# Asking for single packets in the loads of a streaming attention kernel

## The chip, the cores and the metric

The kernel runs on one core of one Trainium2 chip. The metric is device time in microseconds (us) of one execution. Where a run says 363 us, its profile shows a span of 362 us, because the span is taken from the first to the last instruction.

## The reference, cut to what matters

Two independent problems, A and B, are computed and joined. Each is one decode step of attention with a sliding window, two batches, 16 KV heads of width 128, two query heads for each, and the last 4,096 positions of the cache:

```
q = x @ wq                                   # x: [2, 1, 576], wq: [576, 4096]
k, v = the last W = 4096 positions of k_cache, v_cache   # bf16
p = softmax(q k^T * 128**-0.5)
o = p v
out = o @ wo                                 # wo: [4096, 576]
```

There is one query for each sequence, so every byte of K and V is used for very little arithmetic. K and V are 134 MB, wq and wo 19 MB, 153 MB together. The kernel is a stream of loads with computing beside it.

## The kernel before: the parts that matter

All big loads are issued from SyncE ("sp"), on one queue. K and V of four heads of one batch go into one of four ring slots of 4 MB. In SBUF a slot has 128 partitions of 32 KB, and each partition's 32 KB are contiguous in HBM, so a transfer is 128 rows of 32 KB, eight for each of the 16 DMA engines (the trace has 3,968 records of 32,768 B for 31 such transfers; the last V is cut in three). A transfer is issued when its slot is free (`deps`), and its semaphore counts 16.

```
def issue(key):
    ...
    src = src_t[b, 4 * g:4 * g + 4, Sk - W:Sk, :].rearrange("k (r j) d -> r k j d", j=KJ)
    r = slot_of[key]
    prior = uses[r][:uses[r].index(key)]
    deps = [last_reader[prior[-1]]] if prior else first_deps[r]
    cuts = [(0, KJ, ring_sem[r])]                 # one transfer; the last V is cut in three
    ...
    for c0, c1, sm in cuts:
        def f(e, c0=c0, c1=c1, sm=sm):
            return e.dma_start(ring[:, r, c0 * 128:c1 * 128],
                               src[:, :, c0:c1, :].rearrange("r k j d -> r k (j d)")).then_inc(sm, 16)
        stream_dma[key].append((c0, c1, dma_op("sp", sm, 1, f, deps, ...)))
```

wo is loaded in the same way in pieces of up to 18,432 B a row. wq (36,864 B a row) opens the stream. x is tiny and comes on ScalarE's queue ("act"):

```
x:   e.dma_start(x4[2 * h:2 * h + 2, P, :], probs[P][0][:, 0, :]).then_inc(x_sem[P], 16)     # act
wq:  e.dma_start(ringf[:, P * QW:(P + 1) * QW], src).then_inc(wq_sem[P], 16)                 # sp
```

## Time and profile before

| what | before |
|---|---|
| time, median | 363.09 us |
| DMA rate, mean over the span | 424 GB/s |
| share of 16 DMA engines' span taken by the load queue | 98.7% |
| VectorE busy, TensorE busy | 60%, 66% |

First some lines of the page of the kernel before. The line "DMA" is the busy share of the DMA engines in tenths, one digit for each fortieth of the span. Then come the packet count, the load queue and ScalarE's queue (packets, MB, share of 16 engines' span), and the engines' shares of the chain that ended last.

```profile
DMA  8999999999999999999999999999999999999996
DMA packets 6227, 153.26 MB, mean 424 GB/s; under 512 B 700, under 2 KB 840, under 8 KB 1224
q1 hardware_dynamic: 6196, 153.10, 98.7%
q10 hardware_dynamic: 20, 0.01, 0.0%
DMA 48%; DVE 26%; PE 16%; issue 8%; ACT 1%; POOL 0%; SPq 0%
```

In every slice but the two at the ends the DMA engines are at least 90% busy. The trace's packet records say it more sharply: at every moment from 3 to 357 us at least 16 packets are under way, as many as there are engines. Next, the windows view of the kernel before in four stretches of the stream. A line gives the stretch in us and its length, then the busy us (and instructions) of TensorE, its weight loads, VectorE, ScalarE and GpSimd. The last three numbers are the granted TensorE clock (the share of its full clock that TensorE was allowed in that stretch), the DMA engines' busy share and GB/s.

```profile
25.00:100.00 75.00, 52.08 (x229) 10.72 (x129) 50.95 (x20) 8.44 (x18) 4.72 (x18) 0.89 1.01 433
100.00:200.00 100.00, 65.96 (x361) 16.11 (x267) 61.22 (x38) 15.02 (x24) 5.65 (x20) 0.83 1.00 430
200.00:300.00 100.00, 69.25 (x372) 17.02 (x273) 64.52 (x43) 10.42 (x17) 5.08 (x19) 0.83 1.00 431
300.00:343.00 43.00, 29.36 (x180) 8.14 (x144) 27.16 (x24) 10.00 (x16) 2.07 (x8) 0.80 1.00 428
```

A share of 1.00 or 1.01 at 428 to 433 GB/s: there is no hole in the stream to fill. Last, two groups of the DMA issues of the kernel before (transfers, KB each, median us from issue to landing):

```profile
ring<-in_A_k_cache_dram SPq DMA_DIRECT2D x8, 4096.0 KB, 24.3
ring<-in_A_v_cache_dram SPq DMA_DIRECT2D x8, 4096.0 KB, 29.9
```

At 431 GB/s, 4,096 KB take 9.7 us. A transfer that lands 24 to 30 us after its issue therefore had one or two others ahead of it. The computing keeps the queue filled. The chain's 26% for VectorE lies in stretches in which that queue was still full.

The trace also has the records that the page counts as packets. The 6,196 of the load queue are one for each row (5,506; eight for each engine and transfer) and one for each semaphore write (690 of 4 B, a median 9 ns; 16 for each transfer). From their durations (4,096 B in 159 ns, 36,864 B in 1,364 ns, medians) comes the line rate, 1.177 ns for 32 B, and a constant of 8.4 ns a row. By this estimate, that constant is all of a row's time that joining rows could save.

### The profile page before, as it was taken

How to read it: one execution, taken by the hardware profiler on the slowest of the kernel's cores; microseconds unless marked ns; L12 is line 12 of the kernel's file. 1: busy time of each engine (PE TensorE's matmuls, PEld its weight loads, DVE VectorE, ACT ScalarE, POOL GpSimd, SP SyncE). 2: the span in 40 equal slices, each digit the busy share in tenths (PEclk: the TensorE clock that was granted, in tenths of full speed). 3: DMA queues.
4: the chain of work that ended last, by engine and by line, in shares of the span. 5: the costliest groups of instructions: out<-in, count | busy, mean ns of one | idle time of the engine just before them, and what ended most of it. 6: DMA issues, size and time to landing. Idle time of an engine off the chain costs nothing.

```text
span 361.8 us, 2625 instructions
## 1 busy us (share of the span) xinstructions
PE 240.2 (66%) x1292; PEld 57.2 (16%) x927; DVE 218.7 (60%) x150; ACT 46.0 (13%) x78; POOL 24.3 (7%) x84
## 2 busy tenths in 40 slices
PE   0497787666485747662596675567776875668695
PEld 0000111112111201111121121112112121112222
DVE  1901898495929591934909585682927776674622
ACT  1002100040023000500005000500005000500500
POOL 4200101100010001000010000100010001000000
PEclk9999698969988996888788796888688796868969
DMA  8999999999999999999999999999999999999996
GB/s 327 457 435 406 460 408 446 424 431 438 417 453 408 457 404 428 444 431 431 435 420 444 417 449 410 440 431 438 424 442 412 449 417 429 435 435 431 417 412 256
DMA packets 6227, 153.26 MB, mean 424 GB/s; under 512 B 700, under 2 KB 840, under 8 KB 1224
## 3 DMA queue, kind: packets, MB, share of 16 engines
q1 hardware_dynamic: 6196, 153.10, 98.7%
q8 instruction: 8, 0.13, 0.1%
q14 instruction: 3, 0.02, 0.0%
q10 hardware_dynamic: 20, 0.01, 0.0%
HBM read 153.10 MB, written 0.00 MB: 423 GB/s over the span
## 4 chain that ended last, share of the span: by engine, by line
DMA 48%; DVE 26%; PE 16%; issue 8%; ACT 1%; POOL 0%; SPq 0%
DMA ring<-in_B_k_cache_dram 17%; DVE xt L433 16%; DMA ring<-in_A_k_cache_dram 13%; DMA ring<-in_B_v_cache_dram 9%; DMA ring<-in_B_wq_dram 7%; PE st L264 5%; PE st L459 5%; DMA wob<-in_B_wo_dram 3%; PE pj L264 2%; DVE oR L566 2%; DVE mx L467 2%; DVE pT L506 2%; DVE tmp L559 2%; PE ot L536 2%; PE pj L618 1%
## 5 line engine op out<-in xcount | busy, mean ns | idle before, releaser
L459 PE MATMUL st<-xt,zq 128*128 128x512 bf16 x256 | 124.1, 485 | 86.1 <-DVE xt L433 86.1
L433 DVE STREAM_TRANSPOSE xt<-ring 128x4096 f32<-128x4096 f32 x32 | 141.5, 4427 | 28.0 <-DMA ring<-in_A_k_cache_dram 18.8
L264 PE MATMUL st<-xt,zq 128*128 128x512 bf16 x256 | 122.7, 479 | 0.0
L497 ACT ACTIVATE pR<-st,bias 128x512 bf16<-128x512 f32 x32 | 40.0, 1414 | 222.9 <-DVE bias L490 222.9
L459 PEld LDWEIGHTS st<-xt,zq 128*128 128x128 bf16 x256 | 29.4, 115 | 210.1 <-issue 107.7
L536 PE MATMUL ot<-ring,pT 128*32 128x512 bf16 x512 | 32.6, 396 | 3.9 <-DMA ring<-in_B_v_cache_dram 3.9
L490 DVE SCALAR_TENSOR_TENSOR bias<-vmask,tb,offm 128x4 f32<-128x4 f32 x8 | 1.8, 223 | 43.0 <-PE tb L487 43.0
L520 DVE TENSOR_REDUCE ssum<-tb 128x2 f32<-128x8 f32 x8 | 1.3, 162 | 36.0 <-PE tb L517 36.0
L425 POOL TENSOR_TENSOR zq<-qs,bmask 128x64 bf16<-128x64 bf16 x32 | 8.7, 293 | 168.1 <-PE st L264 145.8
L506 DVE STREAM_TRANSPOSE pT<-pR 128x2048 bf16<-128x2048 bf16 x8 | 18.4, 2303 | 0.8 <-ACT pR L497 0.7
L279 PE MATMUL ot<-ring,pT 128*32 128x512 bf16 x18 | 7.6, 421 | 15.0 <-DMA ring<-in_A_wq_dram 14.2
L559 DVE SCALAR_TENSOR_TENSOR tmp<-ot,rsb,dmask 128x512 f32<-128x512 f32 x16 | 11.5, 719 | 7.9 <-PE ot L536 7.9
L566 DVE TENSOR_REDUCE oR<-tmp 128x128 f32<-128x512 f32 x15 | 15.6, 1042 | 0.5
L536 PEld LDWEIGHTS ot<-ring,pT 128*32 128x32 bf16 x512 | 12.4, 99 | 19.6 <-DMA ring<-in_B_v_cache_dram 5.5
L618 PE MATMUL pj<-wob,oM 128*2 128x288 bf16 x48 | 12.7, 299 | 0.0
L264 PE MATMUL pj<-wob,oM 128*2 128x288 bf16 x48 | 12.7, 299 | 0.0
L264 PE MATMUL pj<-ring,pT 128*32 128x512 bf16 x36 | 11.9, 416 | 0.0
L467 DVE TENSOR_REDUCE mx<-st 128x2 f32<-128x1024 f32 x8 | 9.7, 1213 | 0.1
L497 ACT ACTIVATION_READ_ACCUMULATOR pR<-st,bias 128x1 f32 x32 | 8.8, 276 | 0.0
L264 PE MATMUL st<-ring,pT 128*32 128x512 bf16 x18 | 7.3, 407 | 0.0
L222 DVE TENSOR_TENSOR xt<-xt,hmask 4x1152 bf16<-4x1152 bf16 x2 | 2.7, 1349 | 6.7 <-DMA xt<-in_A_x_dram 6.7
L469 POOL TENSOR_TENSOR mv<-mx,v 128x2 f32<-128x2 f32 x8 | 1.6, 195 | 75.8 <-DVE mx L467 75.8
(68 smaller groups left out, 75.6 us busy)
## 6 DMA issues: line engine op xcount, KB each, us to landing
ring<-in_A_k_cache_dram SPq DMA_DIRECT2D x8, 4096.0 KB, 24.3
ring<-in_A_v_cache_dram SPq DMA_DIRECT2D x8, 4096.0 KB, 29.9
ring<-in_B_k_cache_dram SPq DMA_DIRECT2D x8, 4096.0 KB, 27.0
ring<-in_B_v_cache_dram SPq DMA_DIRECT2D x7, 4096.0 KB, 29.8
ring<-in_A_wq_dram SPq DMA_DIRECT2D x1, 4608.0 KB, 13.3
ring<-in_B_wq_dram SPq DMA_DIRECT2D x1, 4608.0 KB, 23.8
wob<-in_A_wo_dram SPq DMA_DIRECT2D x2, 2304.0 KB, 28.3
wob<-in_B_wo_dram SPq DMA_DIRECT2D x1, 2304.0 KB, 27.4
```

Of the source, the lines that this page charges most:

```text
L264: return e.add_instruction(mybir.InstMatmult(name=nc.get_next_instruction_name(), engine=mybir.EngineType.PE, ins=[e.lower_ap(mv_), e.lowe ...
L279: last = e.matmul(QB[c], wt, mv_, start=first, stop=True, skip_group_check=True)
L425: last = e.tensor_tensor(dst, src, msk, ALU.mult)
L433: Xop[(t, jh)] = dve(lambda e: e.transpose(xt[:, jh, :].bitcast(FP32).rearrange("p (kp x kt) -> p x kp kt", kp=2, kt=2), ring[:, r, jh * H ...
L459: last = e.matmul(ob, wt, mv_, start=first, stop=True, skip_group_check=True)
L467: ch[(G, "max")] = dve(lambda e: e.tensor_reduce(mx[:], st[:, :].rearrange("p (x t) -> p t x", t=2), AX.X, ALU.max), [Sop[(2 * G + 1, 1)]] ...
L497: last = e.activation(pR[:].rearrange("p (x k) -> p k x", k=4)[:, kv, :], st[:, :].rearrange("p (x t) -> p t x", t=2)[:, kv % 2, :], ACTF.Exp,
L506: pT_op[G] = dve(lambda e: e.transpose(pT[:, v, :].rearrange("p (w j q) -> p j w q", w=4, q=8), pR[:].rearrange("p (j w q) -> p j w q", w= ...
L536: last = e.matmul(OTB[32 * c:32 * c + 32, :], pT[:, v, base + 32 * c:base + 32 * c + 32], ring[:, r, jj * 128:(jj + 4) * 128], start=rd == ...
L559: evac_op[i] = dve(lambda e: e.scalar_tensor_tensor(tv, o, rsb[:, v, b:b + 1], dm, ALU.mult, ALU.mult), deps, "ev%d" % i)
L566: ch[(G, "red%d" % b)] = dve(lambda e: e.tensor_reduce(oR[:, b, :], tmp[:].rearrange("p (j d) -> p d j", j=4), AX.X, ALU.add), [evac_op[i] ...
L618: last = e.matmul(PJ[h], oM[:, j, :], mv_, start=start and j == 0, stop=True, skip_group_check=True)
```

## The change

The intent is to have the eight rows that one engine moves for a transfer, and its semaphore write, form one packet in place of nine, to save a cost for each packet. Its whole diff is one keyword in two places, for wo and for K and V. wq is left alone.

```
-    rows[:, j0:j1, :].rearrange("p j n -> p (j n)")).then_inc(sm, 16)
+    rows[:, j0:j1, :].rearrange("p j n -> p (j n)"), single_packet=True).then_inc(sm, 16)
...
-    src[:, :, c0:c1, :].rearrange("r k j d -> r k (j d)")).then_inc(sm, 16)
+    src[:, :, c0:c1, :].rearrange("r k j d -> r k (j d)"), single_packet=True).then_inc(sm, 16)
```

## The prediction

> **What bounds the kernel now.** The DMA engines. The page's DMA row is 9 in nearly every slice, and its queue list gives the one load queue 98.7% of 16 engines' span. The windows view gives a DMA share of 0.96 to 1.05 in every 10 us stretch from 10 us to 350 us, at 408 to 455 GB/s. Transfers of 4,096 KB land a median 24 to 30 us after issue (the DMA issues), though one needs only about 9.7 us at 431 GB/s, so two to three are always queued. VectorE is busy 60%, TensorE 66%; the chain of waits gives 26% to VectorE, but in stretches where the queue is still full. The load queue runs without a hole from 1.7 to 359.2 us; about 2.2 us follow (last matmuls, output store).
>
> **What a packet costs.** In the trace's packet records each row is one record, each completion semaphore another (4 B, 9 ns). Median durations: 4,096 B 159 ns, 32,768 B 1,216 ns, 36,864 B 1,364 ns. From the first and last: 1.177 ns per 32 B plus a constant of 8.4 ns. Of a 32 KB row that is 0.7%; the rest is the line rate[...]. 153.1 MB over 16 engines at 1.177 ns per 32 B is 352 us (an estimate from these records), against 357.5 us seen.
>
> [...] whether it belongs to the packet or the row, this trace cannot say.
>
> **What the change does.** No instruction moves on any engine; bytes, rows, waits and order are the same. Per DMA engine, K, V and wo are 328 rows and 41 semaphore writes: 369 packets become 41. If the whole 8.4 ns goes with the packet, 328 x 8.4 ns = 2.8 us is saved, all critical, since the queue is never empty. If the constant is per row, nothing[...]. wq stays as it is, so the x loads between its packets (5 to 13 us) are untouched.
>
> **What it may cost.** [...] A packet grows from 32 KB (1.2 us) to 256 KB (about 9.7 us, estimated from eight records). Eight 16 KB instruction fetches run between the loads, at 53, 109, 148, 191, 233, 273, 309 and 340 us; each may come up to 9 us later. They are some 40 us apart[...].
>
> **Prediction.** 361.5 us, 360.0 to 363.4 us. Faster by over 2%: 0.03 (the line rate leaves no more); within 2%: 0.93; slower by over 2%: 0.04.
>
> **What the profile should show.** Mean GB/s from 424 to about 426; windows 1 to 3 GB/s higher; fewer packet records if the profiler counts packets, the same 6,227 if it counts rows; per-row time nearer 1,205 ns; landings still 24 to 30 us; the same chain; PE busy unchanged.
>
> **What would make it wrong.** A bubble at the end of each large packet[...]; instruction fetches that starve TensorE[...].

The "it" in the third paragraph is the constant of 8.4 ns. The sizes that remain for the saving are 2.8 us and nothing. The centre, 361.5 us, is 1.6 us under the 363.09 us of before. "Up to 9 us later" is the author's estimate from eight records of 1,216 ns.

## The result, and the profile after

The median is 363.16 us (363.11 to 363.45, 4 runs) against 363.09 us (363.07 to 363.26, 4 runs). The ratio is 1.0003, with a 95% interval of 0.9985 to 1.002. Ratios in this document are the mean time of one kernel's fast runs over that of the other's fast runs of the same rounds, so they are not quite the ratio of the medians quoted. No change can be seen.

The lines of the page of the kernel after that answer to those shown of before:

```profile
DMA  8999999999999999999999999999999999999996
DMA packets 6227, 153.26 MB, mean 423 GB/s; under 512 B 700, under 2 KB 840, under 8 KB 1224
q1 hardware_dynamic: 6196, 153.10, 98.7%
q10 hardware_dynamic: 20, 0.01, 0.0%
DMA 49%; DVE 24%; PE 16%; issue 8%; ACT 1%; POOL 1%; SPq 0%
```

The windows view of the kernel after, in the same four stretches:

```profile
25.00:100.00 75.00, 52.30 (x228) 10.71 (x128) 51.07 (x20) 8.44 (x18) 4.72 (x18) 0.89 1.00 433
100.00:200.00 100.00, 62.31 (x365) 15.60 (x267) 62.62 (x38) 15.02 (x24) 5.65 (x20) 0.90 1.00 430
200.00:300.00 100.00, 64.70 (x368) 16.42 (x272) 63.12 (x43) 10.41 (x17) 4.93 (x19) 0.86 1.00 431
300.00:343.00 43.00, 28.35 (x180) 8.00 (x144) 27.19 (x24) 10.04 (x16) 2.21 (x8) 0.84 1.00 429
```

And its DMA issues:

```profile
ring<-in_A_k_cache_dram SPq DMA_DIRECT2D x8, 4096.0 KB, 24.7
ring<-in_A_v_cache_dram SPq DMA_DIRECT2D x8, 4096.0 KB, 29.8
```

The packet count, the rate in each stretch and the landings are the same. The median 32 KB row takes 1,216 ns in both traces. TensorE's busy time does differ between the two profiles, 240 us before and 230 us after, with another granted clock (0.849 and 0.887). The first experiment shows that this is no effect of the change.

Three theories were to be told apart:

- **A**: packets of eight rows are formed on the chip, but the 8.4 ns belong to each row and stay.
- **B**: no packets of eight are formed. The request is lost on its way, and the chip does the same as before.
- **C**: DMA time is saved, but something else sets the kernel's time. The equal row times already speak against it.

One comparison needs no chip. Both kernels were compiled by the same compiler, and the compiled instruction streams compared. The program that goes into the compiler differs (the transfers of K, V and wo carry the request). What comes out does not; the first twelve digits of each stream's hash:

```
engine    before         after          wq asked too
SyncE     eb5d5b820376   eb5d5b820376   eb5d5b820376
TensorE   da0b290508ce   da0b290508ce   da0b290508ce
VectorE   d9e7a22b3c96   d9e7a22b3c96   d9e7a22b3c96
ScalarE   50942a6487e6   50942a6487e6   50942a6487e6
GpSimd    1e036cfb94c2   1e036cfb94c2   1e036cfb94c2
```

All the other files packed into the two compiled programs were equal too. That is theory B at its source: the compiler used here accepts the request and encodes nothing for it. (With the V loads issued from GpSimd, streams with and without the request came out equal as well; that kernel was not run.) Kernels 3 and 4 below are one compiled program in the same way, and so are 5 and 6. So a pair with and without the request is one program run twice, and what differs within a pair is spread. The experiments ask whether what the chip did agrees, and whether the rest of the prediction's argument holds.

### The profile page after: what moved, and what is told of

Its sections match the earlier page's. It is cut to its first block, busy times and chain, and to the rows that moved or that the text cites. A ratio compares the mean times of both kernels' runs of the same rounds, so it can differ in the third digit from the quotient of the medians.

```text
span 361.9 us, 2626 instructions
## 1 busy us (share of the span) xinstructions
PE 230.2 (64%) x1293; PEld 55.8 (15%) x927; DVE 218.8 (60%) x150; ACT 46.0 (13%) x78; POOL 24.3 (7%) x84
## 2 busy tenths in 40 slices
DMA packets 6227, 153.26 MB, mean 423 GB/s; under 512 B 700, under 2 KB 840, under 8 KB 1224
## 4 chain that ended last, share of the span: by engine, by line
DMA 49%; DVE 24%; PE 16%; issue 8%; ACT 1%; POOL 1%; SPq 0%
DMA ring<-in_B_k_cache_dram 25%; DVE xt L433 15%; DMA ring<-in_B_v_cache_dram 9%; DMA ring<-in_B_wq_dram 7%; DMA ring<-in_A_k_cache_dram 6%; PE st L264 6%; PE st L459 6%; DMA wob<-in_B_wo_dram 3%; DVE oR L566 2%; DVE mx L467 2%; DVE pT L506 2%; PE pj L264 2%; DVE tmp L559 2%; PE ot L536 1%; ACT pR L497 1%
## 5 line engine op out<-in xcount | busy, mean ns | idle before, releaser
L459 PE MATMUL st<-xt,zq 128*128 128x512 bf16 x256 | 118.7, 464 | 94.1 <-DVE xt L433 94.1
L264 PE MATMUL st<-xt,zq 128*128 128x512 bf16 x256 | 117.6, 459 | 0.0
L459 PEld LDWEIGHTS st<-xt,zq 128*128 128x128 bf16 x256 | 28.2, 110 | 211.2 <-DVE xt L433 110.5
L536 PEld LDWEIGHTS ot<-ring,pT 128*32 128x32 bf16 x512 | 12.4, 99 | 22.3 <-DMA ring<-in_B_v_cache_dram 9.1
L264 PE MATMUL pj<-wob,oM 128*2 128x288 bf16 x48 | 12.0, 286 | 0.0
L618 PE MATMUL pj<-wob,oM 128*2 128x288 bf16 x48 | 12.0, 286 | 0.0
L279 PEld LDWEIGHTS ot<-ring,pT 128*32 128x32 bf16 x18 | 1.8, 103 | 30.8 <-DMA ring<-in_A_wq_dram 14.9
```

The source lines that it names most:

```text
L264: return e.add_instruction(mybir.InstMatmult(name=nc.get_next_instruction_name(), engine=mybir.EngineType.PE, ins=[e.lower_ap(mv_), e.lowe ...
L279: last = e.matmul(QB[c], wt, mv_, start=first, stop=True, skip_group_check=True)
L459: last = e.matmul(ob, wt, mv_, start=first, stop=True, skip_group_check=True)
L536: last = e.matmul(OTB[32 * c:32 * c + 32, :], pT[:, v, base + 32 * c:base + 32 * c + 32], ring[:, r, jj * 128:(jj + 4) * 128], start=rd == ...
L618: last = e.matmul(PJ[h], oM[:, j, :], mv_, start=start and j == 0, stop=True, skip_group_check=True)
```

## The experiments

All eight kernels ran. Seven gave correct results; the eighth is wrong.

**1. The kernel before once more** (no edit).

> The kernel before once more, unchanged, as a control: how far two profiles and times of one program differ. All theories: 363.1 us, ratio 1.000. Median time of a 32,768 B row 1,216 ns. If single differences between the traces of before and after (first landings 0.8 us later, granted clock 0.887 against 0.849) show up here too, they are not the change's.

Measured: 363.07 us (4 runs), ratio 0.9996 (0.9981 to 1.0011). The busy line of this second profile of the kernel before:

```profile
PE 230.4 (64%) x1293; PEld 55.9 (15%) x927; DVE 218.5 (60%) x150; ACT 46.0 (13%) x78; POOL 24.4 (7%) x84
```

TensorE is busy 230.4 us here, with no change in the kernel, at a clock of 0.882. So the 240 against 230 us between the profiles of before and after is the spread of one program from run to run. It cost nothing: the two profiled runs of this program took 363.01 us (with 240 us of TensorE) and 363.06 us.

**2. wq as single packets too.**

```
-  e.dma_start(ringf[:, P * QW:(P + 1) * QW], src).then_inc(wq_sem[P], 16)
+  e.dma_start(ringf[:, P * QW:(P + 1) * QW], src, single_packet=True).then_inc(wq_sem[P], 16)
```

> The change, and the two wq transfers as single packets too[...]. Theory A (the packets are formed, but the 8.4 ns constant belongs to each row): [...]x lands 20 to 40 us later than now (last x semaphore at 12 to 13 us), the q matmuls start late, the time rises by 10 us or more, above 373 us. Theory B (no packet of eight is formed at all; the request is lost before the chip): the x records stay about 1.4 us apart, x lands by 13.5 us, 363.1 us, ratio 1.000.

The 20 to 40 us of theory A are the author's estimate, from eight rows of 1,364 ns.

Measured: 363.16 us, ratio 0.9999 (0.9984 to 1.0014). What VectorE waited for x, in the waits of the kernel before:

```profile
DVE xt L222 <- DMA xt<-in_A_x_dram: 6.7, 1, 6.7
```

and in the waits of this kernel:

```profile
DVE xt L222 <- DMA xt<-in_A_x_dram: 5.7, 1, 5.7
```

x comes no later. Experiment 1, the kernel before once more, had 5.6 us here, so the 1.0 us between the two lines is spread. The packet records of ScalarE's queue say the same (start in us; an x row is 1,152 B, a semaphore 4 B). In each kernel one of the two interleaved sequences of records is listed:

```
before:        row 5.28, sem 6.69, row 8.05, sem 9.46, row 10.82, sem 12.23
wq asked too:  row 5.33, sem 6.74, row 8.10, sem 9.51, row 10.88, sem 12.28
```

Successive items are 1.36 to 1.41 us apart. One wq row takes 1,364 ns (median); eight would take 10.9 us. The two queues take turns row by row, with the request and without it. What a joined packet would do to these turns was not shown here, so this tells that the request changed nothing, and not how the rows are grouped in packets.

**3 and 4. Rows of 4 KB, without and with the request.** This makes the disputed constant large: each K and V transfer becomes eight transfers of 4 KB rows on the same semaphore. Kernel 4 is the same edit of the kernel after. The cut below leaves out the count of the semaphore, which follows.

```
+  for s0 in range(c0, c1, 16):
+      last = e.dma_start(ring[:, r, s0 * 128:(s0 + 16) * 128],
+                         src[:, :, s0:s0 + 16, :].rearrange("r k j d -> r k (j d)")).then_inc(sm, 16)
```

> The kernel before with each K and V transfer cut into transfers of 4 KB rows: per DMA engine 2,048 rows in place of 272, and 256 semaphores in place of 34. If the 8.4 ns constant is real and all DMA time is critical: 1,776 x 8.4 ns + 222 x 9 ns = 16.9 us more, 380.0 us (377 to 383). If DMA time is not what sets the kernel's time (theory C, a saving is hidden by another limit): clearly less than that.

> The same 4 KB rows with the change's single packets for K, V and wo. If packets are formed and the constant belongs to the packet (what the prediction hoped for): nearly all of the 16.9 us comes back, 362 to 365 us. Theory A (packets formed, constant per row) and theory B (no packets formed): the same as without, 380.0 us, ratio of the two 1.000, 4,096 B rows at 159 ns in both.

Measured: 380.48 us without and 380.38 us with, against 363.24 us for the kernel before in the same rounds; ratios 1.0478 (1.046 to 1.0495) and 1.0476 (1.046 to 1.0491). Packet count, and the stretch from 100 to 200 us in the windows view, without the request:

```profile
DMA packets 38197, 153.29 MB, mean 404 GB/s; under 512 B 4252, under 2 KB 4392, under 8 KB 37416
100.00:200.00 100.00, 60.33 (x349) 15.23 (x261) 56.50 (x36) 12.54 (x21) 5.48 (x19) 0.85 1.03 410
```

The same two lines with the request:

```profile
DMA packets 38197, 153.29 MB, mean 404 GB/s; under 512 B 4252, under 2 KB 4392, under 8 KB 37416
100.00:200.00 100.00, 61.41 (x341) 15.34 (x257) 54.79 (x36) 10.91 (x17) 5.47 (x19) 0.83 1.03 410
```

The engines are just as full (share 1.03) but deliver 410 GB/s in place of 430. The rise of 17.24 us was forecast at 16.9. Solved for the constant: (17.24 us - 222 x 9 ns) / 1,776 rows = 8.6 ns a row. The request brings none of it back: a saving for each packet would have shown as some 15 us here (an estimate: 1,776 rows x 8.4 ns). The 4,096 B row takes a median 161 ns in both (159 was expected).

These two cannot tell A from B: under A the cost of a row would stay as well. They rule out that the request formed packets and saved their cost.

**5 and 6. A small load amid the stream, without and with the request.** It goes from ScalarE's queue, whose loads of x took turns with the big queue in experiment 2 (1.36 to 1.41 us between items).

```
+  if G == 1:
+      dma_op("act", probe_sem, 1,
+             lambda e: e.dma_start(scr[:], probs[0][2][0, 0, 0:128, 0:64]).then_inc(probe_sem, 16),
+             [exp_op[G]], "probe")
```

> The kernel before with one more small load (128 rows of 128 B, eight rows and one semaphore on each DMA engine) issued from ScalarE's queue after the second group's exponentials, amid the stream. Each of its rows takes turns with the big queue. Rows of 1.2 us as packets: it lands after about 9 turns, 8 to 14 us. This is the yardstick for the next run; time unchanged within 1 us.

> The same small load beside the change's single packets. Theory A (packets of eight rows are formed, 9.7 us each[...]): the load lands after up to 9 turns of 9.7 us, 40 to 90 us. Theory B (no packets of eight): 8 to 14 us, as in the run without.

Measured, one look each and so without a state: 363.38 us and 363.32 us. The probe's line in the DMA issues, beside rows that were not asked to be joined:

```profile
scr<-in_A_v_cache_dram ACTq DMA_DIRECT2D x1, 16.0 KB, 14.5
```

and beside the change's transfers:

```profile
scr<-in_A_v_cache_dram ACTq DMA_DIRECT2D x1, 16.0 KB, 14.2
```

14.5 and 14.2 us are a hair over the 8 to 14 us expected, and far from the 40 to 90 us of theory A, which are the author's estimate (nine turns of eight 1,216 ns rows). (The expectation left out the 3.4 and 3.9 us that pass between the start of the issue and the first record.) The load's records run from 114.6 to 125.3 us in the first and from 112.8 to 122.7 us in the second, eight rows and a semaphore taking about nine turns with 32 KB rows (1.216 us each). Turns of 9.7 us were not seen. That a joined packet would have been one turn was the author's assumption for both experiments with two queues (2 and 6) and was not shown here; the equal instruction streams do not rest on it.

**7. Rows of 8 KB.** The edit is that of experiment 3 with 32 in place of 16 (16 where the cut of the last V is not a multiple of 32).

> As the kernel with 4 KB rows, but 8 KB: per DMA engine 1,040 rows of K and V in place of 272, 130 semaphores in place of 34. A constant of 8.4 ns per row: 768 x 8.4 ns + 96 x 9 ns = 7.3 us more, 370.4 us (369 to 372); so 0.43 of what the 4 KB rows cost.

Measured: 370.63 us against 363.19 us in the same rounds, ratio 1.0206 (1.0191 to 1.0221). That is 7.44 us more, 0.43 of the rise with 4 KB rows, and (7.44 us - 96 x 9 ns) / 768 rows is again 8.6 ns. Its packet count:

```profile
DMA packets 20052, 153.28 MB, mean 414 GB/s; under 512 B 2236, under 2 KB 2376, under 8 KB 3144
```

With both row sizes the cost comes to the same constant for each row, and the kernel pays it in full.

**8. Rows 512 B shorter** (a wrong result; the relative error was 0.27).

```
-  cuts = [(0, KJ, ring_sem[r])]
+  cuts = [(0, KJ - 2 if prior else KJ, ring_sem[r])]
```

> Wrong result on purpose: 27 of the 32 K and V transfers leave out their last 2 of 128 columns, so their rows are 32,256 B and old data is used for the rest; nothing else moves. Saves 27 x 8 x 512 B per DMA engine, 216 x 18.8 ns = 4.1 us of DMA time, somewhat more than the change was predicted to save. If a saving in DMA time reaches the end (theories A and B): 359.0 us (358.3 to 359.7). Theory C (a saving of this size is hidden by another limit): 361 us or more.

Measured: 359.34 us against 363.19 us, ratio 0.9896 (0.988 to 0.9913), 3.85 us less. Packet count and one stretch of its windows:

```profile
DMA packets 6227, 151.49 MB, mean 423 GB/s; under 512 B 700, under 2 KB 840, under 8 KB 1224
100.00:200.00 100.00, 62.37 (x339) 15.05 (x244) 62.59 (x38) 15.05 (x24) 5.65 (x20) 0.86 1.00 431
```

A saving of 4.1 us in DMA time gave 3.85 us at the end. So a saving of 2.8 us would have been seen: theory C falls. Had the change taken anything near its intended cost away, the time would have shown it.

**Verdict.** Theory B, in that the request is lost on its way. The compiled streams are equal, and nothing that the chip showed in eight runs tells a kernel with the request from one without. Theory A in the strict sense was never tried: the request changed no program here, so what it would save if it reached the chip stays open. How the chip groups rows in packets without it is not shown either. No experiment gave a correct kernel that beats both.

## Why the prediction was wrong

The prediction said 361.5 us, a small gain. The measured median of 363.16 us lies in its range (360.0 to 363.4) and in the class it gave 0.93, but the gain that it named did not come. Point by point:

- **"What bounds the kernel now. The DMA engines."** Right. Shares of 1.00 to 1.01 in all four stretches shown of the stream, and changes of DMA time in both directions arrived at the end: 17.24 us for 16.9 forecast, 7.44 for 7.3, 3.85 for 4.1.
- **"a constant of 8.4 ns"**. Right in size: 8.6 ns from two kernels with other row sizes. It was read from two sizes in one trace, before anything ran.
- **"369 packets become 41"**. This is the step that failed. It was taken from the words of the change. In its place, the two kernels compiled to equal instruction streams, the chip took 363.16 us against 363.09 us, and two queues took turns after every single row (1.36 to 1.41 us between items beside rows of 1,364 ns), with the request as without it. The term "328 x 8.4 ns = 2.8 us is saved" should have been zero.
- **"If the constant is per row, nothing"** named the right number by luck, for a reason that was not the cause. The prediction weighed where a constant belongs, and did not ask whether the request takes effect at all. Compiling both kernels and comparing the streams would have settled the case before any estimate.
- **"What it may cost"**: packets of 9.7 us that make other queues wait. Not seen: the request changed nothing, and with it x's items still came 1.36 to 1.41 us apart. The 9.7 us were an estimate from eight rows of 1,216 ns. It neither stands nor falls.
- **"Mean GB/s from 424 to about 426"**, row time near 1,205 ns: not so (423 and 1,216 ns). "The same 6,227 if it counts rows" came true, but it had been given an excuse in advance and so could show nothing.
- **"PE busy unchanged"** was no test either: the same program gave 240 and 230 us in two profiles.

## What to carry to other kernels

Before costing a change that is a flag, find out whether it reaches the compiled program: equal streams are one program, whatever the flag is called. If a saving is small and disputed, enlarge the thing that it saves on: 4 KB rows turned a disputed 2.8 us into a cost of 17 us, and made the answer plain. In this stream, which fills the DMA engines, each row cost its bytes plus about 8.6 ns. So long rows are worth keeping here, and by that estimate rows of 32 KB (1,216 ns) have only 0.7% left to give.
